# A second Strassen level for the down product of the later experts, with outputs added up by accumulating transfers

## Chip, cores, metric

One core of a Trainium2 chip (the experiments ran on three chips, each with its own runs of the kernel before). The metric is the device time of one execution in microseconds (us), as the median of several executions. The kernel before takes 1806.56 us (three runs, 1805.99 to 1806.63).

## The reference

Attention without softmax, an RMS norm, then a mixture of four experts whose outputs are all used. All is f32.

```python
kv  = einsum('bhsd,bhse->bhde', k, v)             # 8 x 8 heads, S 576, d 64
x   = rms_norm(einsum('bhsd,bhde->bhse', q, kv)) * g_norm   # -> [4608, 512]
p   = domain_probs / (domain_probs.sum(-1) + 1e-9)
for e in range(4):                                # D = 512, F = 1024
    h = maximum(x @ w1[e], 0)                     # up product
    out += p[:, e:e+1] * (h @ w2[e])              # down product
```

The kernel works in 36 steps: 4 experts times 9 chunks of 512 tokens.

## The kernel before

Strassen's method computes a 2 x 2 block product with seven block products in place of eight, at the price of additions. The kernel has two such levels in the up product (49 small products) and one in the down product (7). The additions of blocks ("combinations", `combine`) may run on VectorE or on GpSimd (`either`). The kernel makes its own schedule: each operation is entered with a key (its place in the order), a cost for each engine that may do it, and what it reads and writes. `layout` then simulates the engines and gives every engine one fixed order. On the chip each engine runs its order, and semaphores are put in only for data.

An addition on VectorE with both inputs in SBUF (the memory that holds the kernel's tiles) and an addition on GpSimd exclude each other (in e12 below one that takes 0.36 us takes 0.62, as it waits for GpSimd's). What they compete for is called the shared port here. The planner knows it: operations with `port=True` never overlap in the plan.

```python
def ready(op, eng):                # in Plan.layout: when could op start on eng?
    ...
    if op.port:
        when = max(when, port)     # end of the last operation with port=True
    return when

def combine(key, cost, out_, a, b, op, reads, writes):
    plan.add(
        key, cost,
        lambda eng: adder(eng).tensor_tensor(out=out_(), in0=a(), in1=b(), op=op),
        reads=reads, writes=writes, port=True,
    )
...
order = plan.layout(slots, idle, ("u1", "u2", "db"), 0.0)
with tc.manual_schedule(engines={ENG.PE, ENG.DVE, ENG.Activation, ENG.Pool, ENG.SP}):
    ...
    for op in order:
        op.fn(op.eng)              # nothing here carries the port exclusion to the chip
```

In the up product every group of seven small products goes through a few banks of PSUM (where the kernel has TensorE's products written), and VectorE has to empty them in time:

```python
def total(a, t, src, add_, whole=whole, key=key):     # sum out of PSUM, VectorE only
    plan.add(key - 0.4, dve(HN),
        lambda eng: nc.vector.tensor_tensor(
            out=block(whole, a, t), in0=src.ap[:, 0:HN], in1=add_.ap[:], op=ALU.add),
        reads=[src, add_], parts=[whole])
```

The down product with one level, and its way of adding up the output over the experts:

```python
for i in range(NR):                                   # earlier experts' sum from scratch
    acc[i] = Buf("small", f"acc{s}_{i}")
    if e:
        load(..., acc[i], lambda i=i: acc[i].ap[:], out_kept[c, i][:], 256, ...)
...
for t in range(2):
    for j, m in enumerate(ORDER):                     # 7 products, 256 columns
        for kt in range(4):
            nc.tensor.matmul(ps.ap[:, 0:HN], lhsT=four(h[m])[:, kt // 2, t, kt % 2, :],
                rhs=w2f[e][m].ap[:, kt * HN:(kt + 1) * HN], ...)
        merge(...)                                    # VectorE: acc = ps * prob + acc
    store(...)                                        # to scratch, to out for the last expert
```

## Time and profile before

| | before |
|---|---|
| time, us | 1806.56 |
| TensorE (PE) busy, us, share of span | 1788.7, 99% |
| VectorE (DVE), ScalarE (ACT), GpSimd (POOL) busy, us | 1010.0, 614.3, 582.0 |
| TensorE's waits for other engines | about 10 us in all |

How to read it: TensorE is never short of work, so a change counts by what it takes from TensorE's own instructions, if the others keep up. The prediction shows the lines of the page for this. One view it only tells is TensorE's waits. Of the kernel before (what waits, for what, total us, how often, longest us), its two longest lines and the first one of the up product (the others are left out):

```profile
PE ab L549 <- DVE small L465: 2.5, 2, 1.8
PE u L927 <- POOL ident masks.py:199: 1.3, 1, 1.3
...
PE u L745 <- DVE big L769: 0.6, 2, 0.3
```

L549 is attention, L927 the start. The up product (L745) waits for the sums out of PSUM (L769) twice in the whole run, 0.6 us together.

### The profile page before, as it was taken

How to read it: one execution, taken by the hardware profiler on the slowest of the kernel's cores; microseconds unless marked ns; L12 is line 12 of the kernel's file. 1: busy time of each engine (PE TensorE's matmuls, PEld its weight loads, DVE VectorE, ACT ScalarE, POOL GpSimd, SP SyncE). 2: the span in 40 equal slices, each digit the busy share in tenths (PEclk: the TensorE clock that was granted, in tenths of full speed). 3: DMA queues.
4: the chain of work that ended last, by engine and by line, in shares of the span. 5: the costliest groups of instructions: out<-in, count | busy, mean ns of one | idle time of the engine just before them, and what ended most of it. 6: DMA issues, size and time to landing. Idle time of an engine off the chain costs nothing.

```text
span 1803.8 us, 31919 instructions
## 1 busy us (share of the span) xinstructions
PE 1788.7 (99%) x12626; PEld 1667.9 (92%) x12626; DVE 1010.0 (56%) x1757; ACT 614.3 (34%) x1345; POOL 582.0 (32%) x447
## 2 busy tenths in 40 slices
PE   8999999999999999999999999999999999999998
PEld 8899999999989999999999999999999999999997
DVE  5765565556565555555565555555565555555553
ACT  3534444443232333333333333333332333333331
POOL 4855555546445211111155111111144211111112
PEclk9999999999999999999999999999999999999999
DMA  9855454323343333343445333334444334344321
GB/s 229 250 188 138 129 170 154 113 97 141 134 141 129 129 129 129 129 128 123 157 147 169 118 120 127 124 123 129 152 161 167 122 124 129 129 129 129 128 96 35
DMA packets 163286, 247.78 MB, mean 137 GB/s; under 512 B 51009, under 2 KB 92225, under 8 KB 163137
## 3 DMA queue, kind: packets, MB, share of 16 engines
q1 hardware_dynamic: 163136, 245.75, 42.6%
q8 instruction: 99, 1.62, 0.4%
q14 instruction: 51, 0.41, 0.1%
HBM read 172.56 MB, written 73.14 MB: 136 GB/s over the span
## 4 chain that ended last, share of the span: by engine, by line
PE 97%; DVE 1%; POOL 1%; SPq 1%; DMA 0%; ACT 0%; issue 0%; POOLq 0%; DVEq 0%; ACTq 0%
PE u L745 44%; PE db L882 30%; PE ab L882 18%; PE ab L539 1%; PE ab L521 1%; PE ab L549 1%; PE ab L506 1%; SPq L310 1%; PE ab L588 0%; DMA big<-in_v_dram 0%; PE u L927 0%; POOL big L304 0%; DVE big L304 0%; POOL rt L458 0%; PE ab L603 0%
## 5 line engine op out<-in xcount | busy, mean ns | idle before, releaser
L304 POOL TENSOR_TENSOR big<-big,big 128x1024 f32<-128x1024 f32 x136 | 323.7, 2391 | 1005.9 <-DVE big L304 815.0
L882 PE MATMUL db<-big,big 128*128 128x256 f32 x2520 | 594.6, 379 | 0.7 <-POOL big L304 0.7
L882 PEld LDWEIGHTS db<-big,big 128*128 128x128 f32 x2520 | 455.7, 190 | 50.8 <-POOL big L304 1.1
L745 PEld LDWEIGHTS u<-xf,big 128*128 128x128 f32 x3600 | 470.2, 192 | 20.9 <-issue 0.9
L761 ACT ACTIVATE snap<-u 128x256 f32<-128x256 f32 x756 | 290.1, 384 | 585.3 <-PE u L745 497.2
L745 PE MATMUL u<-xf,big 128*128 128x128 f32 x3600 | 486.1, 276 | 0.1
L769 DVE TENSOR_TENSOR big<-u,snap 128x256 f32<-128x256 f32 x756 | 314.8, 422 | 240.0 <-PE u L745 124.0
L304 DVE TENSOR_TENSOR big<-big,big 128x1024 f32<-128x1024 f32 x292 | 372.9, 1278 | 31.4 <-ACT big L728 13.3
L745 PE MATMUL u<-xf,w1y 128*128 128x128 f32 x2700 | 357.1, 275 | 0.7 <-DVE big L769 0.6
L882 PE MATMUL ab<-big,big 128*128 128x256 f32 x1512 | 357.4, 379 | 0.0
L745 PEld LDWEIGHTS u<-xf,w1y 128*128 128x128 f32 x2700 | 334.6, 192 | 5.8 <-DVE big L769 1.0
L882 PEld LDWEIGHTS ab<-big,big 128*128 128x128 f32 x1512 | 273.3, 190 | 29.8
L839 DVE SCALAR_TENSOR_TENSOR small<-db,p_all,small 128x256 f32<-128x256 f32 x243 | 117.2, 482 | 247.6 <-PE db L882 247.3
L761 ACT ACTIVATE big<-u 128x256 f32<-128x256 f32 x252 | 96.8, 384 | 413.3 <-PE u L745 410.9
L728 ACT ACTIVATE big<-big 128x1024 f32<-128x1024 f32 x144 | 151.8, 1054 | 71.7 <-DVE big L304 60.3
L839 DVE SCALAR_TENSOR_TENSOR small<-ab,p_all,small 128x256 f32<-128x256 f32 x189 | 91.1, 482 | 149.5 <-PE ab L882 149.4
L835 DVE TENSOR_SCALAR small<-db,p_all 128x256 f32<-128x256 f32 x72 | 34.7, 482 | 70.3 <-PE db L882 63.9
L458 POOL TENSOR_TENSOR rt<-ss,mhalf 128x8 f32<-128x8 f32 (+1 forms) x40 | 66.1, 1652 | 3.3
L304 POOL TENSOR_TENSOR xf<-xf 128x128 f32<-128x128 f32 (+1 forms) x74 | 47.8, 656 | 17.6 <-DVE xf L304 15.2
L449 DVE TENSOR_REDUCE ss<-small 128x8 f32<-128x512 f32 (+1 forms) x40 | 27.1, 679 | 22.4 <-ACT small L444 22.3
L454 POOL TENSOR_SCALAR ss<-ss 128x8 f32<-128x8 f32 (+1 forms) x40 | 9.3, 232 | 77.2 <-DVE ss L449 75.8
L745 PE MATMUL u<-small,big 128*128 128x128 f32 x216 | 33.6, 280 | 0.6 <-ACT snap L761 0.5
(83 smaller groups left out, 744.3 us busy)
## 6 DMA issues: line engine op xcount, KB each, us to landing
xf<-x SPq DMA_DIRECT2D x108, 512.0 KB, 3.4
o<-small SPq DMA_DIRECT2D x108, 256.0 KB, 2.1
small<-o SPq DMA_DIRECT2D x108, 256.0 KB, 4.2
xf<-x_h SPq DMA_DIRECT2D x81, 256.0 KB, 3.4
xf<-x SPq DMA_DIRECT2D x81, 256.0 KB, 3.6
x<-xf SPq DMA_DIRECT2D x36, 512.0 KB, 3.2
big<-in_moe_w_dram SPq DMA_DIRECT2D x32, 512.0 KB, 5.8
small<-in_q_dram SPq DMA_DIRECT2D x72, 128.0 KB, 4.1
```

What stands on the lines that cost most here:

```text
L304: lambda eng: adder(eng).tensor_tensor(out=out_(), in0=a(), in1=b(), op=op),
L310: key, SPC, lambda eng: nc.sync.dma_start(out=dst(), in_=src), reads=reads,
L449: lambda eng: nc.vector.reduce_sum(out=ss.ap[0:n, :], in_=rows(sq), axis=AX.X),
L458: nc.gpsimd.tensor_tensor(out=rt.ap[0:n, :], in0=ss.ap[0:n, :], in1=mhalf[0:n, :], op=ALU.pow)
L506: nc.tensor.transpose(bank.ap[:, rs], qt.ap[:, rs], ident[:])
L728: lambda eng: nc.scalar.activation(out=b.ap[:], in_=b.ap[:], func=ACT.Relu),
L745: nc.tensor.matmul(ps.ap[:, u * P:(u + 1) * P], lhsT=w1f[e][m][mm][1]()[:, u * P:(u + 1) * P], rhs=views[m][mm][1](), start=(mm in (1, 2, ...
L761: lambda eng: nc.scalar.activation(out=where(), in_=ps.ap[:, 0:HN], func=ACT.Copy),
L769: lambda eng: nc.vector.tensor_tensor(out=block(whole, a, t), in0=src.ap[:, 0:HN], in1=add_.ap[:], op=ALU.add),
L835: nc.vector.tensor_scalar_mul(out=acc[i].ap[:, cols], in0=ps.ap[:, 0:HN], scalar1=prob)
L839: nc.vector.scalar_tensor_tensor(out=acc[i].ap[:, cols], in0=ps.ap[:, 0:HN], scalar=prob, in1=acc[i].ap[:, cols], op0=ALU.mult, op1=ALU.add,)
L882: nc.tensor.matmul(ps.ap[:, 0:HN], lhsT=four(h[m])[:, kt // 2, t, kt % 2, :], rhs=w2f[e][m].ap[:, kt * HN:(kt + 1) * HN], start=(m in (1, ...
```

## The change

Its intent is to take an eighth of the products out of the down product where there is room for the additions: in chunks 1 to 7 of the experts 1 to 3, 21 of 36 steps. Each of the seven outer products is computed by seven inner ones of 128 columns, two outer products at a time side by side in one bank. This needs quarter forms of `w2` (28 combinations for each expert), forms of `h` for each chunk, and additions to put the results together. ScalarE takes over copies and the scaling by the probability. But for the very last step, the sum over the experts isn't loaded and stored any more: GpSimd sends each part with an accumulating transfer, which adds to what lies in memory, into `out` (112 sends). The buffers get more room.

```diff
+    def down_deep(s, e, c):
+        for i, group in enumerate(((1, 6), (7, 5), (4, 2), (3,))):
+            for o, m in enumerate(group):              # 3 combinations: forms of h
+                combine(at - 0.3, either(NT), ...)
+                for to, a, sub in ((2, 3, 0), (3, 2, 2)):
+                    combine(at - 0.29, either(HN), ...)
+            for j, mm in enumerate(ORDER):             # 7 inner products
+                for o, m in enumerate(group):
+                    for kt in range(2):
+                        nc.tensor.matmul(ps.ap[:, o * P:(o + 1) * P], ..., rhs=w2q[e][m][mm]...)
+                # ScalarE copies 1, 6, 7, 4; VectorE sums 2, 7, 3 out of PSUM
+            add(...)                                   # 1 to 3 recombinations, port=True
+            out_(...)                                  # scale by the probability
+            send(key, ...)
 ...
-            load(..., acc[i], ..., out_kept[c, i][:], 256, ...)
+                    if e and not again:
+                        nc.gpsimd.dma_start(out=dst, in_=cell(i)[parts, :], accum_op=ALU.add)
 ...
+    def weights_2(...):  def inner(): ...              # 28 combinations an expert
 ...
-            down(s, e, c)
+            if c == 1 and e:
+                inner[e]()
+            if e and 1 <= c < NCH - 1:
+                down_deep(s, e, c)
+            else:
+                down(s, e, c)
```

Cut: new layout of the buffers and their re-use late in the run, another order of the products in `down`.

## The prediction

> **What bounds the kernel now.** I read the page's busy shares first, then the slices, the chain that ended last, and windows of one chunk.
>
> ```profile
> span 1803.8 us, 31919 instructions
> PE 1788.7 (99%) x12626; PEld 1667.9 (92%) x12626; DVE 1010.0 (56%) x1757; ACT 614.3 (34%) x1345; POOL 582.0 (32%) x447
> PEclk9999999999999999999999999999999999999999
> PE 97%; DVE 1%; POOL 1%; SPq 1%; DMA 0%; ACT 0%; issue 0%; POOLq 0%; DVEq 0%; ACTq 0%
> ```
>
> TensorE is busy for 99% of the span, it runs at full clock, and 97% of the chain is its own matmuls following each other. A busy TensorE alone proves little, so I looked at one chunk of a later expert (a window of 46 us) and at what TensorE waits for:
>
> ```profile
> 1200.00:1246.00 46.00, 46.00 (x310) 43.11 (x309) 24.95 (x43) 14.76 (x32) 7.04 (x3) 1.00 0.39 125
> 900.00:946.00 46.00, 46.00 (x310) 43.11 (x309) 29.65 (x53) 14.50 (x32) 26.14 (x22) 1.00 0.47 150
> ```
>
> The columns are length, then busy time of PE, weight load, DVE, ACT and POOL, the clock and the DMA share. TensorE has no gap in either window, not even in the second, where the next expert's weights are being combined. The waits of TensorE over the whole run sum to under 10 us. So the time is the sum of the matmuls' own durations, and a change is worth what it takes from that sum, as long as the other engines keep up.
>
> The chain in order of time gives the price of a matmul where the stream is dense:
>
> ```profile
> 436.23 3.12 PE u L745 x28
> 439.35 1.73 PE db L882 x8
> ...
> 1785.40 6.91 PE db L882 x32
> 1792.31 6.92 PE ab L882 x32
> ```
>
> L745 is the up product (128 columns an instruction): 3.12/28 = 0.1114 us. L882 is the down product (256 columns): 6.91/32 = 0.216 us. An f32 matmul of the program is two such instructions.
>
> **What the Trainium skill says.** (1) "TensorE: Matmul & The Clock Gate", section "Back-to-back issue gap": an isolated matmul costs N/2.4 + 2.5 ns, so a fixed part comes with each instruction. The trace has twice the columns for f32: 106.7 + 4.7 ns and 213.3 + 2.8 ns, so two halves cost 2 x 0.1114 - 0.216 = 7 ns more than one whole. (2) The same page, section "LDWEIGHTS", puts a weight load of 128 columns at about 107 ns. That would just fit under 0.1114 us, with almost no margin; the bursts of 28 up products show that it does. (3) "SBUF — State Buffer", section "Who interferes with whom": a VectorE instruction with two SBUF inputs and a GpSimd instruction that reads SBUF exclude each other for the whole instruction. The trace agrees:
>
> ```profile
> 976.80 5.64 POOL L304 TENSOR_TENSOR big<-big,big 128x1024 f32<-128x1024 f32 x2
> 980.46 3.06 DVE L304 TENSOR_TENSOR big<-big,big 128x1024 f32<-128x1024 f32 x1
> ```
>
> GpSimd's pair ends at 982.44; the VectorE addition, 1.22 us when alone, takes 3.06 us and ends at 983.52. (4) "DMA: Bandwidth & Descriptors", section "SWDGE vs HWDGE vs iDMA": accumulating transfers must be issued from GpSimd, which writes the descriptors in software. The kernel before has no such transfer, so nothing in its trace prices one.
>
> **The change, part by part.** It touches the down product of chunks 1 to 7 of experts 1 to 3: 21 of 36.
>
> *TensorE.* Removed per chunk: 7 products x 4 x 2 token halves = 56 matmuls of 256 columns = 112 instructions x 0.216 = 24.20 us. Added: 7 outer x 7 inner x 2 = 98 matmuls of 128 columns = 196 x 0.1114 = 21.84 us. The saving is 2.36 us a chunk, not the eighth of 24.2 (3.0 us) that the count of products promises, because narrow instructions pay the fixed part twice as often. Times 21: **49.6 us**. The built order confirms 2058 matmuls of the new kind and 840 of the old; the up product is unchanged. As TensorE is gapless, all of this is on the path. Floor: 1806.6 - 49.6 = 1757.0 us. Start (about 20 us to the first products) and tail (a serial last chunk) stay as they are.
>
> *ScalarE*, per deep chunk: 14.8 us now, plus 12 copies of 256 columns at 0.384 us (4.6), 4 of 128 (about 1.1, an estimate from the same row), 8 scalings by the probability that VectorE did (3.1): 23.6 of 43.7 us.
>
> *VectorE*: about 25 now; minus 14 merges x 0.482 (6.75); plus 9 sums out of PSUM x 0.42 and 3 half ones (4.6); plus its part of the new forms of h and of the recombination, in the built order of a typical chunk 7 x 0.417 + 6 x 0.69 (7.1). About 30 of 43.7 us.
>
> *GpSimd*: 7.0 now; plus 7 combinations of 256 at 0.73 (5.1), 8 of 512 at 1.27 (10.2), 4 accumulating sends (about 1 us each, an estimate after the skill's first-byte figure for this path). About 26 of 43.7 us.
>
> None of the three alone reaches TensorE's 43.7 us (21.84 x 2). But VectorE and GpSimd exclude each other for SBUF-only additions. Counting only those, with the uncontested durations above (256: 0.417 and 0.73; 512: 0.69 and 1.27; 1024: 1.22 and 2.36), the built order gives 16.8 + 22.3 = **39 us of exclusive port per deep chunk**, against 16.8 us per ordinary chunk before. Where the second-level forms of w2 are made (28 more combinations per expert) it is 35 us in one chunk and 48 to 50 in the next: 83 to 86 of 89.8 us for the pair. Over the eight chunk times from there to the next expert: about 327 of 352 us, 93%. Port work was 35.3 of 46 us (77%) in the busiest gapless steady chunk before.
>
> *DMA*: 108 loads and the stores of partial outputs to scratch go; 112 accumulating sends take their place. The share of the DMA engines is 0.39 in these windows, so this frees nothing that binds.
>
> **The rivals.**
>
> (a) *The shared port becomes the bound.* For: 93% over a whole expert, in-order engines, and a blocked VectorE also holds back the sums that free the PSUM banks TensorE waits for. Between a product and the next one into the same bank there are, in the built order, typically 3 to 4 other products, 1.3 to 1.8 us; one blocked addition of 3 us is longer. Against: the kernel before already had 3 us blocks without a gap in TensorE, the order is laid out with the exclusion in it, and real durations overlap a little at both ends. If hand-overs cost the port 10%, its 327 us would become 363 against TensorE's 352: 3 x 11 us on top of the floor, 1790, within 2%.
>
> (b) *Accumulating sends hold things up.* The output buffers are shared with the pool of large tiles, and in the built order the next user is, by TensorE's own work between, 3.5 to 9 us behind the send, often 5.7 us and on GpSimd. Landing of a plain 256 KB store takes 2.1 to 2.9 us by the table of DMA issues; two accumulating ones, read and write, perhaps 5 to 6 (estimate). So a late landing would cost GpSimd about 1 us in many chunks, and TensorE only if the port is full. If issue cost 3 us rather than 1, GpSimd would go to 34 of 43.7 and (a) would become likelier: 1775 to 1785.
>
> (c) *Weight loads bound the dense stream.* Now the wide down products give the loader slack (0.190 us per load in 0.216). After, both streams are 128 columns. At 0.118 us an instruction instead of 0.1114, the 21 chunks with 392 instructions each would lose 54 us: all of the gain. The bursts of 28 at 0.1114 speak against it; a few bursts of 32 to 40 at 0.118 to 0.120 are in the trace, but in the attention part, where other waits may be merged in.
>
> **Range and chances.** Floor 1757. I add 2 us for each of the three entries (the 48 to 50 us chunks) and under 0.1 us for each other deep chunk, some 6 us for (a) and (b) together: 1763 us, 2.4% faster. Two percent is 1770.4, that is 13 us of stalls or 0.6 us a deep chunk; the gapless past makes less than that likelier, the 93% keeps it open. I give 0.72 to faster, 0.26 to within 2%, 0.02 to slower. The range is from 1756 (no stall) to 1783 (the port binds for part of each expert).
>
> **What would show it right or wrong.** Right: PE busy near 1739 us; windows of 43.7 us per deep chunk with PE fully busy; new products at 0.111 us; VectorE at some 30, ScalarE at 23, GpSimd at 26 us in such a window; DVE as a releaser of PE only a few us in all. Wrong by (a): PE gaps that end in the sums out of PSUM, with blocked additions of over 2 us before them, and most in the chunk after the w2 forms. Wrong by (b): waits on the transfers to the output, or GpSimd idle behind its own sends. Wrong by (c): no gaps, but instructions dearer than 0.1114 us.

## The result

| | before | after |
|---|---|---|
| time, us | 1806.6 | 1820.3 (4 runs, 1819.67 to 1825.02) |
| ratio | | 1.0082, 95% interval 1.0064 to 1.0099 |

Ratios here and below are the mean time of one kernel's fast runs over the mean of the other's fast runs of the same rounds, so they aren't quite the ratio of the medians quoted.

The predicted 1763 us and its range (1756 to 1783) are missed: the kernel became a little slower. Against the floor of 1757 us there are 63 us too many. The page of the kernel after, in the parts that answer to those of before:

```profile
span 1817.9 us, 36718 instructions
PE 1764.0 (97%) x14390; PEld 1693.5 (93%) x14390; DVE 1211.4 (67%) x1929; ACT 825.7 (45%) x1961; POOL 1085.7 (60%) x898
PEclk9899999999999999999999999999999999999999
PE 88%; DVE 7%; issue 2%; POOL 1%; DMA 1%; ACT 0%; SPq 0%; DVEq 0%; POOLq 0%
```

TensorE's share of the chain fell from 97% to 88%, and VectorE's rose from 1% to 7%. TensorE is still 97% busy, so the busy share hides it. The waits of TensorE say where (same columns as above; L802 is the up product, L966 the down product with one level, L826 a sum out of PSUM, L337 a combination, L818 a copy on ScalarE):

```profile
PE u L802 <- DVE big L826: 16.0, 21, 2.3
PE db L966 <- DVE big L337: 7.6, 4, 3.6
PE u L802 <- DVE big L337: 7.2, 4, 2.1
PE u L802 <- ACT snap L818: 4.4, 4, 1.8
```

What was 0.6 us is now 16.0. The new products L1039 hardly wait at all; it is mostly the unchanged up product that waits. A tally of my own from both traces, the time from the start of one matmul to the start of the next beyond its dense price, gives 25.8 us before and 87.3 us after. The growth of 61.5 us is nearly the whole 63. About 42 us of the 87 are waits for VectorE, 7.5 for ScalarE, 13.5 fell at a reduced clock, and some 0.1 us is lost again at each restart.

Why is VectorE late? It works in order, and its own instructions got longer. This is the timeline of the kernel after near the first change of expert (start, duration, engine, line, operation, out<-in, how many in a row; for PE in brackets the idle time before and what ended it). VectorE, then GpSimd, then TensorE:

```profile
600.77 0.42 DVE L826 TENSOR_TENSOR big<-u,snap 128x256 f32<-128x256 f32 x1
601.30 7.30 DVE L337 TENSOR_TENSOR big<-big,big 128x1024 f32<-128x1024 f32 x1
608.52 0.74 DVE L826 TENSOR_TENSOR big<-u,snap 128x256 f32<-128x256 f32 x2
```

```profile
601.15 0.85 POOL L936 DMA_DIRECT2D out_dram<-big  x1
601.76 1.00 POOL L337 TENSOR_TENSOR x_rem<-big 128x256 f32<-128x256 f32 x1
602.45 0.99 POOL L337 TENSOR_TENSOR x_rem<-small 128x256 f32<-128x256 f32 x1
...
606.55 0.95 POOL L337 TENSOR_TENSOR x_rem<-small,x_rem 128x256 f32<-128x256 f32 x1
```

```profile
608.99 1.27 PE L802 MATMUL u<-xf,w1y 128*128 128x128 f32 x9 [2.12 <-DVE big L826]
```

GpSimd issues a send (L936) and goes on with eight combinations in a row, 601.76 to 607.50. VectorE began a combination at 601.30, which takes 1.22 us when alone. It ends at 608.60, after 7.30 us, when GpSimd's whole row is over. Only then come the two sums out of PSUM, and TensorE has meanwhile run out of banks: 2.12 us idle.

I measured this over the whole run by taking from each of VectorE's SBUF additions its uncontested duration (0.42, 0.69 or 1.22 us for 256, 512 or 1024 columns, and likewise for the few of 128). The rest is **blocked time**: 27.2 us before, with 6 additions blocked for over 1 us (at most 2.2); 196.5 us after, 62 over 1 us (at most 6.07). The number of such additions only went from 404 to 737 on VectorE and from 361 to 700 on GpSimd.

The two kinds of window of 46 us that the prediction used, in the kernel after (columns as there: length, busy PE, PEld, DVE, ACT, POOL, clock, DMA share, GB/s), first in the steady part, then at a change of expert, where the next expert's weights are combined:

```profile
1144.00:1190.00 46.00, 45.97 (x411) 45.78 (x411) 32.63 (x57) 23.07 (x58) 30.86 (x25) 1.00 0.46 113
914.00:960.00 46.00, 40.96 (x325) 38.99 (x324) 37.91 (x57) 20.27 (x52) 32.77 (x23) 0.96 0.51 136
```

Some steady windows are free of gaps, but not all: deep chunks there take 44.9 us on average, where 43.7 was predicted and 46.05 is the time of a chunk before. At the change of expert TensorE loses 5 us in one window and the clock falls. In two short windows there it is seen right behind the wait:

```profile
948.00:950.00 2.00, 0.30 (x2) 0.30 (x3) 2.00 (x4) 0.00 (x0) 0.22 (x1) 1.00 0.84 295
...
952.00:954.00 2.00, 2.00 (x12) 1.93 (x11) 1.56 (x3) 0.57 (x2) 1.59 (x2) 0.54 0.43 46
```

The sends, with the total busy time and ns of one, and the time from issue to landing:

```profile
L936 POOL DMA_DIRECT2D out_dram<-big x102 | 91.6, 1005 | 118.9 <-ACT big L913 66.2
...
out_dram<-big POOLq DMA_DIRECT2D x86, 256.0 KB, 5.3
```

1.0 us to issue and 5.3 us to land: the sizes that rival (b) of the prediction had taken.

### The profile page after: what moved, and what is told of

It is laid out like the page before. It is cut to its first block, busy times and chain, and to the rows that moved or that the text cites. A ratio compares the mean times of both kernels' runs of the same rounds, so it can differ in the third digit from the quotient of the medians.

```text
span 1817.9 us, 36718 instructions
## 1 busy us (share of the span) xinstructions
PE 1764.0 (97%) x14390; PEld 1693.5 (93%) x14390; DVE 1211.4 (67%) x1929; ACT 825.7 (45%) x1961; POOL 1085.7 (60%) x898
## 4 chain that ended last, share of the span: by engine, by line
PE 88%; DVE 7%; issue 2%; POOL 1%; DMA 1%; ACT 0%; SPq 0%; DVEq 0%; POOLq 0%
PE u L802 41%; PE db L966 16%; PE db L1039 13%; PE ab L1039 10%; DVE big L337 4%; PE ab L966 3%; PE ab L595 1%; DVE big L1100 1%; PE ab L577 1%; DVE big L826 1%; PE ab L562 1%; PE ab L605 1%; PE u L1164 1%; DMA out_dram<-big 0%; DVE small L1100 0%
## 5 line engine op out<-in xcount | busy, mean ns | idle before, releaser
L802 PE MATMUL u<-xf,big 128*128 128x128 f32 x3456 | 481.9, 278 | 11.9 <-DVE big L337 7.2
L802 PEld LDWEIGHTS u<-xf,big 128*128 128x128 f32 x3456 | 440.8, 194 | 22.6 <-ACT snap L818 6.9
L826 DVE TENSOR_TENSOR big<-u,snap 128x256 f32<-128x256 f32 x696 | 286.7, 420 | 249.2 <-PE u L802 152.6
L337 DVE TENSOR_TENSOR big<-big,big 128x1024 f32<-128x1024 f32 (+1 forms) x359 | 425.2, 1197 | 32.7 <-ACT big L785 25.2
L818 ACT ACTIVATE snap<-u 128x256 f32<-128x256 f32 x756 | 287.9, 382 | 310.0 <-PE u L802 227.5
L337 POOL TENSOR_TENSOR big<-big,big 128x256 f32<-128x256 f32 (+1 forms) x206 | 329.8, 1610 | 152.4 <-DVE big L337 54.9
L802 PE MATMUL u<-xf,w1y 128*128 128x128 f32 x2700 | 377.5, 277 | 19.5 <-DVE big L826 15.7
L802 PEld LDWEIGHTS u<-xf,w1y 128*128 128x128 f32 x2700 | 339.8, 192 | 27.2 <-DVE big L826 20.1
L966 PE MATMUL db<-big,big 128*128 128x256 f32 x1256 | 297.3, 381 | 7.6 <-DVE big L337 7.6
L966 PEld LDWEIGHTS db<-big,big 128*128 128x128 f32 x1256 | 228.9, 191 | 34.0 <-DVE big L337 8.4
L1064 ACT ACTIVATE snap<-db 128x256 f32<-128x256 f32 x252 | 89.4, 356 | 173.6 <-PE db L1039 166.4
L337 POOL TENSOR_TENSOR big<-big 128x512 f32<-128x512 f32 (+1 forms) x91 | 142.3, 1564 | 43.0 <-ACT big L785 31.3
L936 POOL DMA_DIRECT2D out_dram<-big x102 | 91.6, 1005 | 118.9 <-ACT big L913 66.2
L818 ACT ACTIVATE big<-u 128x256 f32<-128x256 f32 x232 | 88.5, 382 | 103.7 <-PE u L802 100.6
L1039 PE MATMUL db<-big,big 128*128 128x128 f32 x820 | 113.3, 276 | 0.4 <-DVE big L337 0.4
L1039 PEld LDWEIGHTS db<-big,big 128*128 128x128 f32 x820 | 102.0, 192 | 0.7 <-DVE big L337 0.6
L1039 PE MATMUL ab<-kv,big 128*128 128x128 f32 x608 | 87.2, 275 | 0.0
L1039 PE MATMUL db<-kv,big 128*128 128x128 f32 x600 | 84.8, 275 | 0.0
```

The source lines that it names most:

```text
L802: nc.tensor.matmul(ps.ap[:, u * P:(u + 1) * P], lhsT=w1f[e][m][mm][1]()[:, u * P:(u + 1) * P], rhs=views[m][mm][1](), start=(mm in (1, 2, ...
L818: lambda eng: nc.scalar.activation(out=where(), in_=ps.ap[:, 0:HN], func=ACT.Copy),
L826: lambda eng: nc.vector.tensor_tensor(out=block(whole, a, t), in0=src.ap[:, 0:HN], in1=add_.ap[:], op=ALU.add),
L936: nc.gpsimd.dma_start(out=dst, in_=cell(i)[parts, :], accum_op=ALU.add)
L1039: nc.tensor.matmul(ps.ap[:, o * P:(o + 1) * P], lhsT=b.ap[:, col:col + P], rhs=w2q[e][m][mm][1]()[:, kt, :], start=(mm in (1, 2, 5) and o ...
L1064: lambda eng: nc.scalar.activation(out=where(), in_=group_of(ps.ap), func=ACT.Copy),
```

## The experiments

The theories, by the letters of the first expectations. **A**: the order at the shared port. The plan lets one engine at a time have it, the chip doesn't keep that order, so GpSimd takes the port for a whole row and VectorE, with the sums out of PSUM behind it, comes late. **B**: VectorE simply has too much to do. **C**: the accumulating sends are the cost. "Blocked time" is as defined above.

### e1_no_deep: everything but the second level

```diff
-            if c == 1 and e:
-                inner[e]()
-            if e and 1 <= c < NCH - 1:
+            if False:
                 down_deep(s, e, c)
```

> The change without its second level: all 36 down products at one level, the rest of the change kept (sums started by ScalarE, accumulating sends from GpSimd, new buffers). Theory A (VectorE and GpSimd exclude each other for additions in SBUF, the second level's additions fill that port, and VectorE comes late to the sums that free TensorE's banks): without those additions blocked time of VectorE falls back from 196 us to under 40 us and the time is that of before, 1800 to 1812 us. Theory C (the accumulating sends cost the gain): the loss stays, since every send stays, and the time is that of before plus the stalls, 1830 us or more.

Measured: 1816.61 us, ratio 1.0052 (1.0037 to 1.0067), correct. That lies between the two forecasts, so neither came true. The ordinary chunks take 46.06 us with all their sends, as before the change, so a send as such does no harm there. What it loses, it loses at the start, at the changes of expert (2.6 us of TensorE idle at each of two) and in the last chunk. Blocked time is 75.7 us, where A had asked for under 40. So the change costs 10 us even without its point, and the second level, which should bring 49.6 us, brings -3.7.

### e2_fill: GpSimd's additions replaced by fills (wrong)

```diff
-            lambda eng: adder(eng).tensor_tensor(out=out_(), in0=a(), in1=b(), op=op),
+            lambda eng: (nc.gpsimd.memset(out_(), 0.0) if eng == "POOL" and key >= 9 else
+                         adder(eng).tensor_tensor(out=out_(), in0=a(), in1=b(), op=op)),
```

(and the same in the recombinations)

> Wrong result on purpose: from the second expert's weights on, each addition that the plan gave to GpSimd becomes a fill of the same output, which reads nothing from SBUF; same order on every engine, same additions on VectorE, same sends. Theory A: VectorE is no longer blocked, blocked time in experts 1 to 3 falls from 158 us to under 30 us, TensorE's idle time from 48 us to about 15 us and the time to 1760 to 1775 us. Theory B (VectorE has simply too much work in its own order, blocked or not): VectorE's own work is unchanged, so the time stays above 1805 us.

Measured: 1776.04 us, ratio 0.9836 (0.9812 to 0.9859). VectorE has the same instructions in the same order as in the kernel after, but GpSimd doesn't read SBUF any more. Blocked time from there on is zero (longest excess 0.004 us). The Trainium skill says this too ("SBUF — State Buffer", section "Who interferes with whom"): a GpSimd instruction that only writes SBUF doesn't contend. Of TensorE's waits for VectorE little is left:

```profile
PE u L803 <- ACT snap L819: 3.6, 4, 1.4
PE db L967 <- DVE big L338: 3.0, 1, 3.0
PE u L803 <- DVE big L338: 1.9, 4, 0.8
```

The time is 1 us above A's range and far from B's. B falls: VectorE can do all its work in the time. But GpSimd is also faster here (639 us busy against 1086), so this alone doesn't prove A.

### e3_port_order: the planned order of the port, kept on the chip (correct)

The loop at the end makes each operation at the port wait for the one before it in the plan, when that one is on the other engine. Nothing else is touched.

```diff
+        held = None
+        sync = mybir.DependencyInfo(mybir.DependencyClass.Sync, mybir.DependencyReason.DATA)
         for op in order:
-            op.fn(op.eng)
+            made = op.fn(op.eng)
+            if op.port:
+                if held is not None and held[0] != op.eng:
+                    tc.add_manual_dep(made.ins, held[1].ins.name, sync, reason="port")
+                held = (op.eng, made)
```

> Right result: an addition in SBUF waits for the one before it in the plan's order when that is on the other engine, so that GpSimd cannot run ahead and hold the port for several additions in a row. Theory D (what hurts is that the planned order at the port is not kept: runs of up to eight GpSimd additions hold one VectorE addition for 6 us): the longest block falls under 1 us, and the time to 1785 to 1800 us, near what the plan's order allows. Theory A with the sheer sum of port work as the cause: the waits only move ahead of the instructions, 1810 to 1830 us.

Measured: 1778.83 us, ratio 0.9843 (0.9828 to 0.9857), better than the 1785 to 1800 us expected. Some 42 us come back by added waits, with all additions and all sends in place. Blocked time is zero (longest excess 0.013 us). The same place in the run as in the timelines above:

```profile
599.72 0.87 POOL L936 DMA_DIRECT2D out_dram<-big  x1
601.13 0.72 POOL L337 TENSOR_TENSOR x_rem<-big 128x256 f32<-128x256 f32 x1 [0.54 <-DVE big L337]
601.82 0.72 POOL L337 TENSOR_TENSOR x_rem<-small 128x256 f32<-128x256 f32 x1
```

```profile
599.81 1.23 DVE L337 TENSOR_TENSOR big<-big,big 128x1024 f32<-128x1024 f32 x1 [0.41 <-POOL big L337]
602.46 0.96 DVE L826 TENSOR_TENSOR big<-u,snap 128x256 f32<-128x256 f32 x2 [1.42 <-ACT snap L818]
```

GpSimd now waits 0.54 us for VectorE's combination, which takes 1.23 us in place of 7.30, and the sums out of PSUM come early enough that they wait for others. The windows of 46 us, steady and at the change of expert:

```profile
1130.00:1176.00 46.00, 45.97 (x412) 45.78 (x411) 28.30 (x57) 24.09 (x59) 28.64 (x24) 1.00 0.45 105
904.00:950.00 46.00, 43.23 (x354) 41.38 (x355) 30.90 (x63) 22.91 (x58) 26.73 (x21) 1.00 0.55 149
```

TensorE no longer waits for any sum out of PSUM (L826). Its two longest lines of waits are now:

```profile
PE u L802 <- DVE big L337: 4.0, 4, 1.3
PE db L966 <- DVE big L337: 3.9, 2, 3.7
```

For as many instructions (57) VectorE is busy 28.3 us where it was 32.6. Deep chunks of expert 3 take 43.9 us on average (43.7 predicted). At the change of expert 2.8 us of gaps remain.

### e4_plain_stores: plain stores in place of the sends (wrong)

```diff
-                        nc.gpsimd.dma_start(out=dst, in_=cell(i)[parts, :], accum_op=ALU.add)
+                        nc.sync.dma_start(out=dst, in_=cell(i)[parts, :])
```

> Wrong result on purpose: the partial outputs go out as plain stores from the sync queue instead of accumulating sends from GpSimd, plan and order otherwise the same. Theory C: GpSimd loses some 100 us of issuing and the late landings go, the time falls by 20 us or more, to 1800 us or less. Theory A: GpSimd gains 4 us a chunk and its additions come a little earlier, a change of under 10 us, 1810 to 1822 us.

Measured: 1806.6 us, ratio 0.9996 (0.9981 to 1.0011), 13.7 us less than the kernel after. Both expectations miss: C asked for 1800 or less, A for hardly a change. The stalls of 2.1 to 2.3 us in three steps that begin with a row of eight combinations of GpSimd are gone, and the longest block falls from 6.07 to 2.16 us. But blocked time is still 171.8 us, and the loss in the steady part stays. So the sends have a part in it, and not the larger one.

### e5_pool_waits, e6_dve_waits: half of e3 each (correct)

```diff
-                if held is not None and held[0] != op.eng:
+                if held is not None and held[0] != op.eng and op.eng == "POOL":    # e5
+                if held is not None and held[0] != op.eng and op.eng == "DVE":     # e6
```

> Half of the order of e3: only GpSimd waits for the VectorE addition planned before it; VectorE waits for nothing new. Theory D in its sharp form (GpSimd runs ahead of the plan and takes the port first): this half is the working one, 1775 to 1790 us, blocked time of VectorE below half of the 196 us. Rival (both engines must be held): 1795 us or more.

> The other half: only VectorE waits for the GpSimd addition planned before it. Theory D: VectorE's blocks only turn into waits ahead of the instruction, GpSimd still runs ahead, 1812 to 1830 us as the changed kernel. Rival (any order at the port is enough): 1775 to 1795 us.

Measured: e5 1777.95 us, ratio 0.9833 (0.9818 to 0.9848); e6 1832.69 us, ratio 1.0134 (1.0119 to 1.0149). Holding GpSimd back until VectorE has had its turn brings the whole gain of e3, though 110.5 us of blocked time remain (the forecast of under half of 196 us missed). Holding VectorE back makes it worse than no order at all, just above the forecast; and the blocks didn't turn into waits as expected: some 160 us of blocked time remain, in 81 blocks of over 1 us, up to 5.8. So it isn't blocked time as such that costs, but GpSimd running ahead of the plan and taking the port from a combination on which sums out of PSUM are waiting.

### e7_six_ordered: e3 with six deep chunks an expert (correct)

```diff
-            if e and 1 <= c < NCH - 1:
+            if e and 1 <= c < NCH - 2:
```

> e3 with the second level in chunks 1 to 6 instead of 1 to 7, so that the last one no longer meets the next expert's weights. Lost: 3 chunks at 2.36 us, 7 us. If the 8 us of gaps and low clock at each of the two changes of expert in e3 come from the port work piled up there, they go: 1768 to 1776 us. If they come from the weights alone: 1783 to 1788 us.

Measured: 1771.38 us, ratio 0.9798 (0.9782 to 0.9815). This is the fastest of all, correct, and faster than both kernels; whether it is over 2% faster than before the interval doesn't decide. Leaving chunk 7 ordinary gives up 3 x 2.17 = 6.5 us of saving (2.17 us is what e11 below shows a deep chunk to be worth), yet the time falls by 7.4 us against e3. So the deep chunk 7, whose down product lies where the next expert's forms are made, cost some 14 us in stalls. (The whole plan is laid out anew in e7, so this is the price by difference.) The window at the change of expert is free of gaps now:

```profile
898.00:944.00 46.00, 46.00 (x302) 42.90 (x301) 31.30 (x54) 17.70 (x40) 17.82 (x18) 1.00 0.58 155
```

### e8_replanned: e7 with the planner's costs taken from the trace (correct)

```diff
-    CROSS, SAME, LANES = 0.3, 0.06, 8
+    CROSS, SAME, LANES = 0.2, 0.06, 8
-        return {"DVE": 0.17 + 0.00108 * n, "POOL": 0.1 + 0.0025 * n}
+        return {"DVE": 0.15 + 0.00105 * n, "POOL": 0.16 + 0.00215 * n}
```

> e7 with the planner given the durations that the trace shows (VectorE 0.15 us + 1.05 ns, GpSimd 0.16 us + 2.15 ns an element; 0.2 instead of 0.3 us between engines). If the planner's slow GpSimd was what spread the work badly, 1758 to 1770 us, the best of all; if not, as e7 within 4 us.

Measured: 1782.37 us, ratio 0.9858 (0.9844 to 0.9873). A miss: costs nearer to the measured ones gave a worse plan, 11 us slower than e7, with 0.68 us of idle TensorE in each steady chunk (45.0 us). I didn't follow up why.

### e9_before_ordered, e11_no_deep_ordered: the order without the second level (correct)

The loop of e3 in the kernel before (e9), and in e1 (e11).

> Control: the kernel before with the order of e3 at the port. TensorE had no gaps there, so if the order helps only where the second level's additions fill the port, nothing changes: 1803 to 1810 us. If the order gave something by itself (so that e3 is no verdict on the change), 1795 us or less.

> e1 (no second level, the rest of the change) with the order of e3. If the 9.6 us that e1 lost to the kernel before come from the port (the additions for the next expert's weights), they go, 1805 to 1810 us; if from the clock at the start and the new buffers, they stay, 1812 to 1818 us. With e1, e3 and the changed kernel it makes a table of second level by order: the second level is then worth some 30 to 40 us with the order, and costs 4 us without.

Measured: e9 1808.71 us, ratio 1.0006 (0.9991 to 1.0021); e11 1810.45 us, ratio 1.0017 (1.0000 to 1.0034). The added waits are no gain in themselves: the kernel before, with 27 us of blocked time, gets nothing from them. e11 is at the edge of its first forecast: 6.2 us of what e1 lost come back with the order, and 3.0 stay. With e1 and e3 this makes a table of two by two (medians in us; before 1806.6 to 1807.5):

| | port order not kept | kept |
|---|---|---|
| no second level | 1816.6 (e1) | 1810.5 (e11) |
| second level in 21 chunks | 1820.3 (after) | 1778.8 (e3) |

The second level costs 3.7 us without the order and brings 31.7 us with it. With 18 deep chunks it brings more: e7 is 39.1 us below e11, 2.17 us a deep chunk.

### e10_port_alone and e12_port_sends: the port by itself (small kernels, wrong, one run each)

Both let a VectorE addition of 256 columns, two SBUF inputs, arrive while GpSimd does a row of additions on other buffers. e10 has rows without a send and behind an accumulating one, and a row of fills; it comes four times each, after one to three VectorE fills.

```python
if send:
    nc.gpsimd.dma_start(out=rows[sent], in_=acc[:], accum_op=ALU.add)   # e12 also without accum_op
for j in range(count):                                                  # 8 of 256 or 4 of 1024
    nc.gpsimd.tensor_tensor(out=o[:, 0:n], in0=a[:, 0:n], in1=b[:, 0:n], op=ALU.add)
for j in range(delay):
    nc.vector.memset(late[:], 0.0)
nc.vector.tensor_tensor(out=dv[:], in0=a[:, 0:256], in1=b[:, 0:256], op=ALU.add)
```

> Wrong result on purpose, only the port: one VectorE addition of 256 columns (0.42 us alone) that arrives in the middle of a row of GpSimd additions, four times each: eight of 256 without a send before them, eight of 256 right behind an accumulating send, four of 1024 without and with a send, and eight fills behind a send. Expected from the traces so far: without a send VectorE waits for the one GpSimd addition that runs (under 0.8 us with 256, under 2.4 us with 1024); behind a send GpSimd's additions overlap by 0.3 us, the port is not let go between them, and VectorE waits for the rest of the row (3 us and more with 256); fills block nothing. Rival: a send makes no difference, and what was seen came from other waits.

Measured: 0.36 us in all four cases without a send; 4.84, 4.83 and 3.65 us behind one (a fourth arrived before the row and took 0.36); with four of 1024, 0.36 to 0.55 us without and 8.60, 8.60 and 7.41 us with a send (again one before the row); behind a send but with fills, always 0.36. Open remained whether the accumulation matters, and whether the arrivals without a send had fallen between two additions by chance. e12 moves the arrival in six steps of about 0.1 us and adds plain sends from GpSimd.

> A kernel of its own again, wrong on purpose. A VectorE addition of 256 columns with two SBUF inputs arrives at six points in steps of about 0.1 us while GpSimd does a row of additions: eight of 256 without a send, behind a plain GpSimd send, behind an accumulating one; four of 1024 without a send and behind a plain one. Theory P (any GpSimd send does it): behind the plain send the VectorE addition takes 3 to 5 us, and 7 to 8.6 us with 1024 columns, as behind the accumulating one. Theory Q (only the accumulating one does it): behind the plain send at most one GpSimd addition is waited out, under 1.1 us with 256 and under 2.7 us with 1024. Without a send, where the arrival falls at all points of a GpSimd addition: between 0.36 and 1.05 us with 256, between 0.36 and 2.7 us with 1024, if an addition that is running is waited out and no more.

The timeline of e12, no send, then a plain send (L49):

```profile
34.23 5.67 POOL L53 TENSOR_TENSOR po<-a,b 128x256 f32<-128x256 f32 x8
36.67 0.62 DVE L58 TENSOR_TENSOR dv<-a,b 128x256 f32<-128x256 f32 x1
...
75.84 0.56 POOL L49 DMA_DIRECT2D out_dram<-acc  x1 [0.25 <-issue]
76.42 5.48 POOL L53 TENSOR_TENSOR po<-a,b 128x256 f32<-128x256 f32 x8
77.86 4.32 DVE L58 TENSOR_TENSOR dv<-a,b 128x256 f32<-128x256 f32 x1
```

In the first case the row lasts until 39.9 but VectorE is through at 37.29, after 0.62 us: it waits for the one addition that is running and gets in before the next. That next one takes 0.90 us in place of 0.72. In the second it is let in only when the row has ended at 81.90. Over all arrivals into a row: without a send 0.36 to 0.73 us; behind a plain send 3.85 to 4.32 us (five of six; the first plain send of the run didn't do it, 0.36), behind an accumulating one 4.30 to 4.87 us (six of six); four of 1024 behind a plain send 7.66 to 8.41 us (six of six), without 0.36 to 0.55. (Without a send no arrival of e12 fell in the middle of a long addition: all came within 0.5 us of the change from the first to the second, and where the second had just begun by the record, VectorE got through and GpSimd's took up to 3.02 us in place of 2.33.) So a plain send from GpSimd does it too; the accumulation isn't needed. I had taken another sign for the cause: behind an accumulating send each GpSimd addition is recorded as 1.0 us and starts 0.3 us before the previous one ends, in place of 0.72 and 0.03. Behind plain sends it isn't so (0.71 and 0.03), and VectorE is shut out all the same. That overlap is not what shuts it out.

This splits the 62 blocks of over 1 us in the kernel after. Nine of them lie in a row of GpSimd work that began with a send: 26.0 us, of which three rows of eight combinations make 17.7, up to 6.07 each. In the other 53, 90.3 us, no send had gone before in the row; none is over 2.2 us, which is less than one GpSimd combination of 1024 columns (2.36). In e4 there are 60, all of the second kind, up to 2.16. The rule of the small kernels doesn't hold for every row here: behind the send at 757.01 GpSimd does five combinations until 766.78, and a VectorE addition that starts at 761.18 waits for only one of them (1.03 us in place of 0.69).

## Why the prediction was wrong

**The price and the saving held.** The chain of the kernel after in order of time, up products and new down products:

```profile
625.48 4.46 PE u L802 x40
...
637.54 1.79 PE db L1039 x16
```

4.46/40 is 0.1115 us and 1.79/16 is 0.1119 us, predicted 0.1114. So rival (c), the weight loads, is refuted: they keep up at 128 columns. The saving is a little smaller than the 2.36 us a chunk predicted: where nothing stalls, in expert 3 of e3, a deep chunk takes 43.9 us against 46.05 before, 2.15 less, and e7 against e11, which differ in the second level alone, gives 39.1 us for 18 chunks, 2.17 each, predicted 42.5. The fixed part that the prediction read off isn't the same at both widths (4.7 and 2.8 ns), but its sum rests on the measured prices, not on it.

**The loads held, more or less.** In the steady window ScalarE has 23.1 us (predicted 23.6), VectorE 32.6 (30; without the 5.1 us of blocked time in this window 27.5), GpSimd 30.9 (26). The send's issue (1.0 us) and landing (5.3) were as taken for rival (b). PE busy is 1764 us, not 1739: 13.5 us of slow clock are in it; the remaining 11 or so I didn't take apart.

**The step that failed** is the "against" of rival (a): "the order is laid out with the exclusion in it". It is in the plan and is not on the chip. Semaphores carry data dependences alone, so GpSimd starts its combinations as soon as their data are there, ahead of the plan, and has the port when VectorE comes. From this followed the wrong term of the sum: "some 6 us for (a) and (b) together". Measured, (a) and (b) make most of 63 us. (The 363 us of rival (a) is 327/0.9; 327 and a tenth is 360.) The wrong sign was even named in the working: "one blocked addition of 3 us is longer" than the 1.3 to 1.8 us that a bank can wait. That earlier blocks of 3 us had made no gap was taken as evidence, though there were only six of over 1 us then; with 62 it no longer held.

**The size that I had looked at was the wrong one.** I asked whether the sum of work at the port, 93%, fits, and allowed 10% for hand-overs. e3 has the same sum and, but for the changes of expert, fits. What counts is who gets the port when, and whether VectorE's queue of sums stands behind it.

**A term that wasn't there at all**: a row of GpSimd additions right behind a GpSimd send can shut VectorE out to its end. It turns a wait of up to 2.2 us into one of 6, three times in this kernel. e4 prices it at up to 13.7 us of this kernel. Up to, since e4 also takes 1 us of issue for each send from GpSimd.

**Where the 63 us went**, by runs:

| part | us | from |
|---|---|---|
| port order not kept (the sends' rows in it) | 41.5 | after 1820.3 - e3 1778.8 |
| deep chunk 7 beside the next expert's forms | 14 | e3 - e7 + 3 x 2.17 |
| rest of the change, order kept | 3 | e11 1810.5 - before 1807.5 |
| saving of 2.17 us a deep chunk in place of 2.36 | 4 | 21 x (2.36 - 2.17), from (e11 - e7)/18 |
| not assigned | about 1 | remainder |

The prediction did say which signs would prove (a): "PE gaps that end in the sums out of PSUM, with blocked additions of over 2 us before them", most of them around the `w2` forms. The profile showed such gaps, so the mechanism was listed and its size wasn't. The place was a chunk early: the steps in which experts 2 and 3 begin, with the end of the deep chunk 7 in them, take 57.0 and 57.7 us where they took 46.3 before, and the steps after them, with most of the second-level forms, 46.9 where e3 needs 44.3.

**What stays open.** The up product of the second step begins at 86.4 us in the kernel after and at 83.0 before. Early on, the trace of the one has 10.2 us at half clock and that of the other 3.4. The change need not be the cause: e9, which is the kernel before with the waits added, also has 10.2 us at half clock there and begins that product at 86.0. What sets it isn't shown. Why a send makes the following row hold the port isn't shown either, nor why the first plain send of e12 didn't (the first addition of its row took 1.93 us in place of 0.71, and VectorE came during it), nor why only some rows of the kernel after do it. And e8 says that the plan's quality hangs on details that I can't predict.

## What to carry to other kernels

An exclusion that a scheduler assumes must be made a dependency, or the engine that can run ahead will break it; hold back that one engine (here GpSimd), not the one that frees the bottleneck's buffers. When VectorE empties PSUM for a dense TensorE, add up how long its other instructions can be held and compare it with how long a bank can wait; the sum of the loads doesn't tell. Keep GpSimd's sends away from the front of a row of its own SBUF additions, and leave an optimization out where the other work already peaks: six deep chunks beat seven.

## What the Trainium skill lacked or had wrong

- "SBUF — State Buffer", section "SBUF: two separate sides", says that whichever of the two instructions starts first gets the shared ports "for the whole instruction". Without a send e12 agrees (VectorE waits for one running GpSimd addition at most, 0.36 to 0.73 us for an addition of 0.36). Behind a GpSimd send more than one instruction can be held: 3.85 to 4.87 us with eight of 256 columns, 7.66 to 8.41 us with four of 1024. In the kernel after, VectorE even starts first by the record (601.30, the row's first addition 601.76) and is shut out. The page warns that VectorE can starve such sends; I found this reverse effect on no page.
- "TensorE: Matmul & The Clock Gate", section "Why this matters for your kernels", advises no idle gaps of over about 3 us. Staying under that wasn't enough here: in the kernel after the clock fell to 0.54 in a stretch of 2 us behind waits of 2.12 and 0.47 us. The page does tell of frequent short gaps that lower the clock (section "A second HAM failure mode: psum-queue depth-cycling"); only the advice leaves them out.
- "DMA: Bandwidth & Descriptors", section "Specifications", has about 1 us to the first byte for transfers issued from GpSimd. I found no figure there for a whole accumulating transfer: 256 KB took 1.0 us of GpSimd to issue and 5.3 us to land, beside 3.8 us for the plain store to the same place in e4.
- "GPSIMD Engine Reference", section "Elementwise — side-by-side cycle accounting", compares an f32 addition on both engines at 2048 columns only. Uncontested, these runs have VectorE 0.42, 0.69 and 1.22 us and GpSimd 0.73, 1.27 and 2.36 us for 256, 512 and 1024 columns.
